# K and V tiles of a cached-attention decode block: from 4 heads by 32 token groups to 32 heads by 4 token quarters

## The chip, the cores and the metric

The kernel runs on one core of a Trainium2 chip. The metric is the device time of one execution, in microseconds (us).

## The reference, cut to what matters

Two sequences, one new token each, pass through an adaptive layer norm, attention over a cached window of 1024 tokens with 32 heads of 192, an output projection, a second layer norm and a gated feed-forward block. All inputs are bf16.

```python
mod = (silu(c) @ w_mod).reshape(2, 6, 1, 640)               # shifts, scales, gates
h = layernorm(x) * (1 + ca) + sa
q = (h @ wq).reshape(2, 1, 32, 192)
k = k_cache[:, :, 3072:4096, :]                             # (2, 32, 1024, 192)
v = v_cache[:, :, 3072:4096, :]
p = softmax(q k^T * 192 ** -0.5)
x = x + ga * ((p v) @ wo)
h = layernorm(x) * (1 + cb) + sb
x = x + gb * ((gelu(h @ w_gate) * (h @ w_up)) @ w_down)
```

K and V are 25.2 MB each, the weights 26.5 MB. Every byte is used once.

## The kernel before

All loads are issued in a fixed order on one DMA queue, and each waits until its landing place is free. K and V land in a ring of 8 slots of 12 KB per partition. A tile holds 4 heads; each head has 32 partitions, and each partition holds 32 consecutive tokens, which lie in memory as one run of 32 x 192 x 2 = 12,288 B.

```python
HQ = 4; PH = P // HQ; J = W // PH            # 4 heads, 32 partitions each, 32 tokens
NQD = H // HQ; NG = B * NQD                  # 16 groups of (4 heads, one batch)
SLOT = J * Dh                                # 6144 elements = 12,288 B

def ring_src(it):                            # the source of a K or V tile
    # (cut)
    src = A_k_cache if kind == "k" else A_v_cache
    return src[b].rearrange("(i u) s d -> u i s d", u=NQD)[quad, :, K0:Sk, :] \
                 .rearrange("i (p j) d -> p i (j d)", p=PH), SLOT     # (shortened)
```

For each of the 16 groups, DVE multiplies K by the broadcast query in two chunks, PE sums over channels by multiplying with the identity, DVE finishes the sums, and a softmax follows: maximum, transpose, broadcast to 4 head columns, exponential, denominator. The four columns are a masked copy of the weights, one column per head, so PV can be a matmul with 8 weight columns (2 tokens x 4 heads); four such matmuls run side by side in column tiles of 32.

```python
S.op("dve", tensor_tensor(prod[...], ring[:, sl, chunk], qbc[...], mult))        # K * q
S.op("pe",  matmul(bank, lhsT=ident_b, rhs=prod[...]))                           # 6 per chunk
# (cut: maximum, transpose, broadcast)
S.op("act", activation(E_sb[:, z, :, :], Sb_sb, Exp, scale=SCALE, accum_out=denp))
for jp in range(NPAIR):                                                          # PV
    i = jp % NR
    e.matmul(ps[32 * i:32 * i + 2 * HQ, BK_O, 0:ON],
             lhsT=E_sb[:, z, 2 * jp:2 * jp + 2, :], rhs=ring[:, sl, 2 * jp * Dh:(2 * jp + 2) * Dh],
             tile_position=(0, 32 * i))
```

The code above is shortened; the whole kernel follows.

Of the kernel before, what the change touches and what calls it, by code (L numbers as in the profile page):

```python
# [119 lines left out]
def bass_adaLN_cond__sliding_block_cached__geglu_ffn__decode_kernel(  # L120
# [24 lines left out]
    HQ = 4  # L145
    PH = P // HQ
    J = W // PH
    NQD = H // HQ
    NG = B * NQD
# [4 lines left out]
    assert B == 2 and D == KT * P and J * PH == W and NQD * HQ == H and NT * P == NQ  # L154
    assert DD * NT == Dh and DD * H == P and NR * FR == FC and FC * P == F and DR == KT * 32
    assert HQ == NR and DD * NQD == 32
    SCALE = float(Dh) ** -0.5
    EPS = 1e-5
    NEG = 1e30
    JC = 16  # L160
    NCK = J // JC
    GC = 512 // JC
    NCH = Dh // GC
    assert GC * NCH == Dh and NCK == 2
    ON = 2 * Dh
    NPAIR = J // 2

    NS = 8
    SLOT = J * Dh
    WQ_SPLIT = [(0, 2), (2, 3)]  # L170
    WO_SPLIT = [(0, 28), (28, 17), (45, 3)]
    NWQ, NWO = len(WQ_SPLIT), len(WO_SPLIT)
# [4 lines left out]
    HP = P // 2  # L177
    X0 = DD * NQD - 1
    ZW = X0 + P
# [3 lines left out]
    assert NQB * QW == NQD * Dh  # L183
# [3 lines left out]
    with es:  # L187
# [3 lines left out]
        ring = sb("ring", [P, NS, SLOT], BF16)  # L191
        R3N = max(KT * 6 * D, 2 * KT * F + FC * D)
        r3 = sb("r3", [P, R3N], BF16)
        wm_v = r3[:, 0:KT * 6 * D].rearrange("p (k n) -> p k n", k=KT)
        wg_v = r3[:, 0:KT * F].rearrange("p (k n) -> p k n", k=KT)
        wu_v = r3[:, KT * F:2 * KT * F].rearrange("p (k n) -> p k n", k=KT)
        wd_v = r3[:, 2 * KT * F:2 * KT * F + FC * D].rearrange("p (f n) -> p f n", f=FC)
        prod = sb("prod", [P, 4, JC, Dh], BF16)
        qbc = sb("qbc", [P, B, NQD * Dh], BF16)
# [5 lines left out]
        mask_h = sb("mask_h", [P, HQ], F32)  # L205
        bcL = sb("bcL", [1 + HQ, P], F32)
        bcR = sb("bcR", [1 + HQ, 2, HQ], F32)
# [4 lines left out]
        selq = sb("selq", [P, B, P], BF16)  # L212
        ztmp = sb("ztmp", [P, NR, 2, HQ], BF16)
# [16 lines left out]
        S_sb = sb("S_sb", [P, 2, J], F32)  # L230
        Sb_sb = sb("Sb_sb", [P, 2, J, HQ], F32)
        M1 = sb("M1", [P, 2], F32)
        E_sb = sb("E_sb", [P, 2, J, HQ], BF16)
        denp = sb("denp", [P, 2], F32)
        rden = sb("rden", [P, 2], F32)
        On = sb("On", [P, 2, B, ON], BF16)
# [21 lines left out]
        sem_wm = S.sem("d_wm")  # L258
        sem_wg = S.sem("d_wg")
        sem_wu = [S.sem("d_wu%d" % i) for i in range(len(WU_SPLIT))]  # L260
        sem_wd = [S.sem("d_wd%d" % i) for i in range(len(WD_SPLIT))]
        sem_ring = [S.sem("d_ring%d" % i) for i in range(NS)]
# [5 lines left out]
        items = [("wq", k) for k in range(NWQ)]  # L268
        items += [("k", 0)]
        for g in range(1, NG):  # L270
            items += [("k", g), ("v", g - 1)]
        items += [("v", NG - 1)]
        items += [("wo", i) for i in range(NWO)]
        nslots = {("wq", i): -(-n * NQ // SLOT) for i, (_, n) in enumerate(WQ_SPLIT)}
        nslots.update({("wo", i): -(-n * D // SLOT) for i, (_, n) in enumerate(WO_SPLIT)})
        slot_of, before_of, pos = {}, {}, 0
        holder = [None] * NS
        for it in items:
            m = nslots.get(it, 1)
            assert pos + m <= NS  # L280
            slot_of[it] = pos
            before_of[it] = [holder[z] for z in range(pos, pos + m) if holder[z] is not None]
            for z in range(pos, pos + m):
                holder[z] = it
            pos = (pos + m) % NS
        ring_f = ring[:, :, :].rearrange("p s n -> p (s n)")
        ring_state = {"next": 0, "done": set()}

        def ring_key(it):
            return [("ring", z) for z in range(slot_of[it], slot_of[it] + nslots.get(it, 1))]  # L290

        def group(g):
            return divmod(g, B)

        def ring_src(it):
            kind, i = it
            if kind == "wq":
                k0, n = WQ_SPLIT[i]
                return A_wq.rearrange("(p k) n -> p (k n)", k=KT)[:, k0 * NQ:(k0 + n) * NQ], n * NQ
            if kind == "wo":  # L300
                t0, n = WO_SPLIT[i]
                return A_wo.rearrange("(p t) n -> p (t n)", t=NT)[:, t0 * D:(t0 + n) * D], n * D
            quad, b = group(i)
            src = A_k_cache if kind == "k" else A_v_cache
            return src[b].rearrange("(i u) s d -> u i s d", u=NQD)[quad, :, K0:Sk, :].rearrange("i (p j) d -> p i (j d)", p=PH), SLOT

        def declare_ring(consumed=()):
            ring_state["done"].update(consumed)
            while ring_state["next"] < len(items):
                it = items[ring_state["next"]]  # L310
                if not all(h in ring_state["done"] for h in before_of[it]):
                    break
                src, width = ring_src(it)
                o0 = slot_of[it] * SLOT
                S.dma("sp", k_dma(ring_f[:, o0:o0 + width], src), sem_ring[slot_of[it]], writes=ring_key(it), name="ld_%s%d" % it)
                ring_state["next"] += 1

        wm_dma = S.dma("sp", k_dma(wm_v.rearrange("p k n -> p (k n)"), w_mod.rearrange("(p k) n -> p (k n)", k=KT)), sem_wm,
                       writes=["wm"], name="ld_wm")
        declare_ring()  # L320
# [3 lines left out]
        for nm, t in (("scT", scT), ("oT", oT), ("aT", aT)):  # L324
# [16 lines left out]
             reads=["ones_b"], writes=["selg"], name="selg")  # L341
        for b in range(B):
            S.op("pool", lambda e, b=b: e.affine_select(out=selq[:, b, :].rearrange("p (x h) -> p x h", h=HQ),
                                                        in_=ones_b[:, 0:1].unsqueeze(2).broadcast_to([P, PH, HQ]),
                                                        pattern=[[0, PH], [-32, HQ]],
                                                        compare_op=ALU.is_equal, fill=0.0, base=-b, channel_multiplier=1),
                 reads=["ones_b"], writes=[("selq", b)], name="selq%d" % b)
        S.op("pool", lambda e: e.affine_select(out=ztmp[:, :, :, :].rearrange("p i q h -> p i (q h)"),
                                                in_=ones_b[:, 0:1].unsqueeze(2).broadcast_to([P, NR, 2 * HQ]),
                                                pattern=[[-32, NR], [-1, 2 * HQ]],  # L350
                                                compare_op=ALU.is_equal, fill=0.0, base=0, channel_multiplier=1),
             reads=["ones_b"], writes=["ztmp"], name="ztmp")
        S.op("pool", lambda e: e.memset(zsel[:, :, :], 0.0), writes=["zsel"], name="zsel0")
        S.op("pool", lambda e: e.memset(bcL[:, :], 1.0), writes=["bcL"], name="bcL1")
        S.op("pool", lambda e: e.affine_select(out=bcL[:, :].rearrange("k (x h) -> k x h", h=HQ),
                                                in_=ones_f[0:1 + HQ, :].rearrange("k (x h) -> k x h", h=HQ),
                                                pattern=[[0, PH], [-1, HQ]],
                                                compare_op=ALU.is_equal, fill=0.0, base=-1, channel_multiplier=1),
             reads=["ones_f", "bcL"], writes=["bcL"], name="bcLh")
        S.op("pool", lambda e: e.memset(bcL[0:1, :], 1.0), writes=["bcL"], name="bcL0")  # L360
        S.op("pool", lambda e: e.memset(bcR[:, :, :], -NEG), writes=["bcR"], name="bcRn")
        S.op("pool", lambda e: e.affine_select(out=bcR[:, :, :], in_=bcR[:, :, :],
                                                pattern=[[0, 2], [-1, HQ]],
                                                compare_op=ALU.not_equal, fill=0.0, base=-1, channel_multiplier=1),
             reads=["bcR"], writes=["bcR"] + [("bcR", z) for z in range(2)], name="bcRd")

        S.op("dve", lambda e: e.memset(ps[:, 0:4, :], 0.0), writes=[bank(k) for k in range(4)], name="init_Q")
        S.op("dve", lambda e: e.memset(ps[:, 5:8, :], 0.0), writes=[bank(k) for k in range(5, 8)], name="init_O")
# [41 lines left out]
        def ln_mod(tag, opc_idx, s_idx, dst_bf):  # L410
# [7 lines left out]
            def f(e):  # L418
                last = None
                hv = hrow[:, :].rearrange("p (m j) -> p m j", j=KT)  # L420
                for j in range(KT):
                    for i in range(NR):
# [10 lines left out]
             reads=["mask_h"], writes=["maskc"], name="maskc")  # L433
        S.op("dve", lambda e: e.tensor_reduce(out=zsel[:, :, X0:X0 + P].rearrange("p q (h m) -> p q h m", m=32)[:, :, :, 0],
                                              in_=ztmp[:, :, :, :].rearrange("p i q h -> p q h i"), axis=AX.X, op=ALU.max),
             reads=["ztmp", "zsel"], writes=["zsel"], name="zsel")

        mod_pe = []
        for half in range(2):
# [143 lines left out]
        for g in range(NG + 2):  # L583
# [6 lines left out]
            if pp:  # L590
                c_rec(g - 2)
# [147 lines left out]
```

## Time and profile before

| | kernel before |
|---|---|
| time | 188.15 us median of 3 runs (188.1 to 188.38) |
| bytes moved | 77.03 MB |
| K and V | 32 transfers of 1536 KB |
| packets of K and V in the trace | 4096 of 12,288 B, mean 464.3 ns each |

First, lines of the page of the kernel before: the span, busy time by engine, the DMA rows of the 40 equal slices of the span (busy tenths, then GB/s), the packet total, and the shares of the chain of work that ended last.

```profile
span 186.7 us, 2408 instructions
...
PE 106.9 (57%) x1038; PEld 51.9 (28%) x1039; DVE 98.2 (53%) x147; ACT 30.0 (16%) x72; POOL 5.1 (3%) x23
...
DMA  8989998999999999999999999999999999999991
GB/s 296 486 366 437 474 422 379 437 427 427 429 424 427 417 426 432 424 424 425 421 427 427 427 430 421 420 429 424 429 422 424 449 462 422 404 402 428 408 399 51
DMA packets 6518, 77.03 MB, mean 413 GB/s; under 512 B 746, under 2 KB 876, under 8 KB 1516
...
DMA 72%; DVE 16%; PE 5%; ACT 2%; SPq 1%; issue 1%
```

The 16 DMA engines are busy in every slice but the last, so the kernel is bound by its DMA stream. No engine is busy for more than 57% of the span. Next, stretches of time of the same kernel; the columns are the stretch, its length, busy time (and instructions) of PE, PE's weight loads, DVE, ACT and POOL, then the granted clock, the DMA share and GB/s. From 13 to 20 us the first part of wq lands; from 45 to 145 us K and V stream.

```profile
13.00:20.00 7.00, 4.60 (x62) 1.84 (x62) 2.22 (x11) 2.25 (x5) 0.00 (x0) 1.00 1.03 442
45.00:145.00 100.00, 67.93 (x518) 32.88 (x520) 75.85 (x99) 13.21 (x41) 0.00 (x0) 0.96 1.01 425
```

In a short stretch the rate is blurred by packets that cross its edges. Cutting the packets at the edges, by their times in the trace, gives 432.7 GB/s for 13 to 20 us and 425.2 for 45 to 145.

Three groups of instructions of the kernel before (busy time, mean ns of one, then idle time before them and what ended it): the K products, the PV matmuls, and the scaling of the PV result.

```profile
L490 DVE TENSOR_TENSOR prod<-ring,qbc 128x3072 bf16<-128x3072 bf16 x32 | 55.9, 1752 | 16.1 <-DMA ring<-in_A_k_cache_dram 16.1
...
L563 ACT ACTIVATE On<-ps,rden 128x384 bf16<-128x384 f32 x16 | 9.3, 581 | 42.4 <-DVE rden L561 31.9
L551 PE MATMUL ps<-ring,E_sb 128*8 128x384 bf16 x256 | 14.8, 356 | 0.0
```

DVE sits idle for 16.1 us before its K products, waiting for K to land. Last, how K and V are issued (count, size, time from issue to landing), and the moment when the output projection starts (start, duration, instruction, and in brackets what it waited for).

```profile
ring<-in_A_k_cache_dram SPq DMA_DIRECT2D x16, 1536.0 KB, 24.6
ring<-in_A_v_cache_dram SPq DMA_DIRECT2D x16, 1536.0 KB, 24.8
```

```profile
162.24 3.92 PE L622 MATMUL ps<-ring,oT 128*17 128x160 bf16 x112 [2.93 <-DMA ring<-in_A_wo_dram]
```

The output projection waits for its weights, not for attention.

### The profile page before, as it was taken

To read this page: it belongs to the slowest core of one execution; us is meant where nothing else is said; L and a number is where in the kernel's file an instruction comes from. 1 tells how busy PE (TensorE), PEld (TensorE's weight loads), DVE (VectorE), ACT (ScalarE), POOL (GpSimd) and SP (SyncE) were. 2 spreads that over 40 slices of the span, in tenths; PEclk is the share of its full clock that TensorE was granted. 3 is DMA by queue.
4 is the path that set the end of the run, shared out by engine and by line. 5 is a ranking of instruction groups with operands and counts; after the bars stand their busy time and mean duration, and the time that the engine had idled before them with its cause. 6 is when DMAs were issued, how large, how long until landed. Compare 5 with 4: busy or idle time off the path is not lost.

```text
span 186.7 us, 2408 instructions
## 1 busy us (share of the span) xinstructions
PE 106.9 (57%) x1038; PEld 51.9 (28%) x1039; DVE 98.2 (53%) x147; ACT 30.0 (16%) x72; POOL 5.1 (3%) x23
## 2 busy tenths in 40 slices
PE   0015710833876678656649656665576895356472
PEld 0011200211243333322314313333233252355321
DVE  6114000019788889587596595785865934002311
ACT  2022100091020212021012011110110103100610
POOL 8200000000000000000000000000000000000000
PEclk9999999997899999999996999999998558555567
DMA  8989998999999999999999999999999999999991
GB/s 296 486 366 437 474 422 379 437 427 427 429 424 427 417 426 432 424 424 425 421 427 427 427 430 421 420 429 424 429 422 424 449 462 422 404 402 428 408 399 51
DMA packets 6518, 77.03 MB, mean 413 GB/s; under 512 B 746, under 2 KB 876, under 8 KB 1516
## 3 DMA queue, kind: packets, MB, share of 16 engines
q1 hardware_dynamic: 6492, 76.88, 97.6%
q8 instruction: 8, 0.13, 0.3%
q14 instruction: 2, 0.02, 0.0%
q10 hardware_dynamic: 16, 0.01, 0.0%
HBM read 76.88 MB, written 0.00 MB: 412 GB/s over the span
## 4 chain that ended last, share of the span: by engine, by line
DMA 72%; DVE 16%; PE 5%; ACT 2%; SPq 1%; issue 1%
DMA ring<-in_A_k_cache_dram 38%; DMA ring<-in_A_wq_dram 17%; DMA r<-in_B_w_down_dram 17%; DVE prod L490 10%; DVE S_sb L509 4%; PE ps L502 2%; PE ps L467 2%; ACT qbc L483 2%; SPq L266 1%; DVE ps L485 1%; DVE M L512 1%; ACT qrow L474 1%; DVE bcR L519 0%; PE ps L526 0%; PE ps L684 0%
## 5 line engine op out<-in xcount | busy, mean ns | idle before, releaser
L490 DVE TENSOR_TENSOR prod<-ring,qbc 128x3072 bf16<-128x3072 bf16 x32 | 55.9, 1752 | 16.1 <-DMA ring<-in_A_k_cache_dram 16.1
L502 PE MATMUL ps<-prod,ident_b 128*128 128x512 bf16 x192 | 51.5, 411 | 15.7 <-DVE prod L490 15.6
L502 PEld LDWEIGHTS ps<-prod,ident_b 128*128 128x128 bf16 x192 | 17.2, 102 | 40.3 <-DVE prod L490 21.0
L509 DVE TENSOR_REDUCE S_sb<-ps 128x32 f32<-128x1024 f32 x16 | 19.3, 1206 | 0.9 <-PE ps L502 0.9
L526 PE MATMUL ps<-bcR,bcL 5*128 5x4 f32 x32 | 6.3, 264 | 22.3 <-DVE bcR L519 22.3
L563 ACT ACTIVATE On<-ps,rden 128x384 bf16<-128x384 f32 x16 | 9.3, 581 | 42.4 <-DVE rden L561 31.9
L551 PE MATMUL ps<-ring,E_sb 128*8 128x384 bf16 x256 | 14.8, 356 | 0.0
L534 ACT ACTIVATE E_sb<-Sb_sb 128x128 bf16<-128x128 f32 x16 | 5.0, 311 | 57.6 <-DVE Sb_sb L531 57.6
L467 PE MATMUL ps<-ring,hT 128*2 128x512 bf16 x60 | 6.7, 626 | 9.9 <-DMA ring<-in_A_wq_dram 9.0
L526 PEld LDWEIGHTS ps<-bcR,bcL 5*128 5x128 f32 x32 | 4.9, 190 | 26.3 <-DVE bcR L519 26.3
L622 PE MATMUL ps<-ring,oT 128*17 128x160 bf16 x192 | 6.8, 338 | 5.5 <-DMA ring<-in_A_wo_dram 5.5
L477 DVE CAST qrow<-ps 128x512 bf16<-128x512 f32 x1 | 0.7, 692 | 15.8 <-PE ps L467 15.8
L531 DVE TENSOR_TENSOR Sb_sb<-S_sb,ps 128x128 f32<-128x128 f32 x16 | 4.6, 289 | 7.8 <-PE ps L526 7.8
L540 PEld LDWEIGHTS ps<-denp,maskc 128*128 128x128 f32 x32 | 6.9, 218 | 3.6 <-ACT E_sb L534 0.9
L622 PEld LDWEIGHTS ps<-ring,oT 128*17 128x17 bf16 x192 | 6.1, 135 | 6.1 <-DMA ring<-in_A_wo_dram 6.1
L641 DVE TENSOR_TENSOR lnt<-ps,modR 128x160 f32<-128x160 f32 x1 | 0.3, 325 | 13.6 <-PE ps L622 13.6
L551 PEld LDWEIGHTS ps<-ring,E_sb 128*8 128x8 bf16 x256 | 5.0, 87 | 3.2 <-issue 0.7
L467 PEld LDWEIGHTS ps<-ring,hT 128*2 128x2 bf16 x60 | 1.7, 114 | 14.9 <-DMA ring<-in_A_wq_dram 9.9
L540 PE MATMUL ps<-denp,maskc 128*128 128x1 f32 x32 | 5.0, 226 | 0.8 <-ACT E_sb L534 0.8
L383 PE MATMUL ps<-ident_b,crow 2*128 2x2 bf16 x5 | 0.4, 177 | 8.2 <-DMA crow<-in_c_dram 8.2
L576 PE MATMUL ps<-On,zsel 128*128 128x96 bf16 x64 | 4.6, 223 | 0.7 <-ACT On L563 0.7
L514 PE MATMUL ps<-ident_f,M 128*1 128x128 f32 x16 | 4.5, 280 | 0.4 <-DVE M L512 0.4
(81 smaller groups left out, 71.5 us busy)
## 6 DMA issues: line engine op xcount, KB each, us to landing
ring<-in_A_k_cache_dram SPq DMA_DIRECT2D x16, 1536.0 KB, 24.6
ring<-in_A_v_cache_dram SPq DMA_DIRECT2D x16, 1536.0 KB, 24.8
r<-in_w_mod_dram SPq DMA_DIRECT2D x1, 4800.0 KB, 14.1
ring<-in_A_wq_dram SPq DMA_DIRECT2D x1, 4608.0 KB, 32.0
ring<-in_A_wo_dram SPq DMA_DIRECT2D x1, 4480.0 KB, 24.6
ring<-in_A_wq_dram SPq DMA_DIRECT2D x1, 3072.0 KB, 20.6
ring<-in_A_wo_dram SPq DMA_DIRECT2D x1, 2720.0 KB, 23.0
r<-in_B_w_gate_dram SPq DMA_DIRECT2D x1, 1920.0 KB, 25.1
```

The lines of the kernel that those rows point to most:

```text
L467: last = e.matmul(ps[32 * i:32 * i + B, n, :], lhsT=hT[:, k, :], rhs=wv[:, kk, i, n * QW:(n + 1) * QW], start=(k == 0), stop=(k == KT - 1) ...
L490: S.op("dve", lambda e: e.tensor_tensor(out=prod[:, 2 * (g % 2) + ci, :, :], in0=ring[:, sl, ci * JC * Dh:(ci + 1) * JC * Dh].rearrange("p ...
L502: last = e.matmul(o_ap, lhsT=ident_b[:, :], rhs=prod[:, pz, :, t * GC:(t + 1) * GC], start=(t == 0), stop=(t == NCH - 1))
L509: S.op("dve", lambda e: e.tensor_reduce(out=S_sb[:, z, :], in_=ps[:, 2 * z:2 * z + 2, :].rearrange("p k (j c) -> p (k j) c", c=GC), axis=A ...
L526: S.op("pe", lambda e: e.matmul(ps[:, BK_T, P:P + HQ], lhsT=bcL[:, :], rhs=bcR[:, z, :], start=True, stop=True), reads=[("bcR", z), "bcL"] ...
L531: S.op("dve", lambda e: e.tensor_tensor(out=Sb_sb[:, z, :, :], in0=S_sb[:, z, :].unsqueeze(2).broadcast_to([P, J, HQ]), in1=ps[:, BK_T, P: ...
L534: S.op("act", lambda e: e.activation(out=E_sb[:, z, :, :], in_=Sb_sb[:, z, :, :], func=ACTF.Exp, scale=SCALE, accum_out=denp[:, z:z + 1]), ...
L540: S.op("pe", lambda e: e.matmul(ps[:, BK_T, P + 16:P + 17], lhsT=maskc[:, :], rhs=denp[:, z:z + 1], start=True, stop=True), reads=[("denp" ...
L551: last = e.matmul(ps[32 * i:32 * i + 2 * HQ, BK_O, 0:ON], lhsT=E_sb[:, z, 2 * jp:2 * jp + 2, :].rearrange("p j h -> p (j h)"), rhs=ring[:, ...
L563: S.op("act", lambda e: e.activation(out=On[:, quad % 2, b, :], in_=ps[:, BK_O, 0:ON], func=ACTF.Identity, scale=rden[:, z:z + 1]), reads= ...
L576: last = e.matmul(ps[:, BK_OT, 0:B * NT].rearrange("p (b t) -> p b t", b=B), lhsT=zsel[:, jj, x:x + P], rhs=On[:, quad % 2, :, jj * Dh + d ...
L622: last = e.matmul(ps[32 * i:32 * i + RM, BK_M, 0:DR], lhsT=oT[:, t, :], rhs=wv[:, tl, i, :], start=(t == 0), stop=(t == NT - 1), tile_posi ...
```

## The change

The intent is to feed the DMA engines longer runs. All 32 heads now sit side by side with 4 partitions each, and a partition holds a quarter of the window, 256 tokens. A tile is 64 tokens of each quarter, one run of 24,576 B per partition, and a batch is 4 K tiles and 4 V tiles. Everything else follows from that layout: there is one softmax per batch, over 256 columns; the weights for PV are expanded with a mask to 32 columns, one per head, so that a PV matmul has 64 weight columns and only two column tiles run side by side; and since slots of 24 KB and the weights no longer fit apart, one arena of 6 slots holds everything, and w_mod, wq, wo and the feed-forward weights share it with K and V.

```diff
-    HQ = 4
-    PH = P // HQ
-    J = W // PH
-    NQD = H // HQ
-    NG = B * NQD
+    XQ = P // H
+    J = W // XQ
+    TT = 64
+    NTL = J // TT
+    SLOT = TT * Dh
@@ where tiles land
-        ring = sb("ring", [P, NS, SLOT], BF16)
-        r3 = sb("r3", [P, R3N], BF16)
+        NS = 6
+        NAR = NS * SLOT
+        arena = sb("arena", [P, NAR], BF16)
+        place = {("wm", 0): (0, KT * 6 * D), ("wq", 0): (2 * SLOT, wq_n[0]), ("wq", 1): (2 * SLOT + wq_n[0], wq_n[1])}
+        tiles = [("k", 0, t) for t in range(NTL)] + [("v", 0, 0)]
+        for t in range(NTL):
+            tiles += [("k", 1, t)] + ([("v", 0, t + 1)] if t + 1 < NTL else [])
+        tiles += [("v", 1, t) for t in range(NTL)]
+        for n, it in enumerate(tiles):
+            place[it] = ((n + NS - 1) % NS * SLOT, SLOT)
@@ source of a tile
-            return src[b].rearrange("(i u) s d -> u i s d", u=NQD)[quad, :, K0:Sk, :].rearrange("i (p j) d -> p i (j d)", p=PH), SLOT
+            return src[b][:, K0:Sk, :].rearrange("h (x j) d -> h x j d", x=XQ)[:, :, t * TT:(t + 1) * TT, :].rearrange("h x j d -> h x (j d)")
@@ weights of PV (new on DVE) and PV
+                S.op("dve", lambda e, z=z, j0=j0: e.tensor_tensor(out=Em[:, z, :, :], in0=E_sb[:, b, j0:j0 + JE].unsqueeze(2).broadcast_to([P, JE, H]),
+                                                                  in1=maskE[:, :].unsqueeze(1).broadcast_to([P, JE, H]), op=ALU.mult),
-                    last = e.matmul(ps[32 * i:32 * i + 2 * HQ, BK_O, 0:ON],
-                                    lhsT=E_sb[:, z, 2 * jp:2 * jp + 2, :].rearrange("p j h -> p (j h)"),
+                        last = e.matmul(ps[64 * i:64 * i + 2 * H, BK_O, 0:ON],
+                                        lhsT=Em[:, z, 2 * jp:2 * jp + 2, :].rearrange("p j h -> p (j h)"),
... (cut: the softmax per batch, the query broadcast, the selection of the result, bookkeeping)
```

## The prediction

> **What bounds the kernel now: the DMA stream.** The page shows 77.03 MB at a mean of 413 GB/s; the DMA row of the 40 slices stands at 8 or 9 tenths until the last slice. By stretches, 45 to 145 us (K and V streaming) has DMA share 1.01 at 425 GB/s, while DVE is busy 75.9 of 100 us and PE 67.9. The chain of waits is 72% DMA. DVE idles 16.1 us for K landings. Only the first microsecond and the tail after the last w_down landing (183.5 to 186.7 us) are not DMA.
>
> **What the change does to the DMA.** Bytes stay. K and V go from 32 transfers in 4096 packets of 12,288 B to 16 transfers in (I expect) 2048 packets of 24,576 B. The trace has both sizes: a 12,288 B packet takes 460 to 473 ns, mean 464.3; the 128 packets of 24,576 B of the first wq part take 912 ns each, and their stretch (13 to 20 us) runs at 432.7 GB/s. 50.33 MB at 425.2 GB/s is 118.4 us; at 431 to 432.7 it is 116.3 to 116.8. Estimate: 1.6 to 2.1 us less, all on the critical path, since wo, gate, up and down shift forward with it.
>
> **What could give it back.** Partitions now walk 32 heads, 1.5 MB apart, instead of four contiguous head blocks. The Trainium skill ("DMA: Bandwidth & Descriptors", Latency and other measured facts) lists row pitches of large powers of two that slow HBM copies, 512 KiB mildly, 2 MiB strongly. No stretch of this trace has a 1.5 MB pitch; I keep one chance in four that packets take 1 to 4% longer than 912 ns.
>
> **Does the shared arena starve the queue?** I count not. At 7.3 us a tile, K/V runs from 31 to 148 us. DVE per K tile: 4 products of 1752 ns and 2 sums of 1206 ns, 9.4 us. Queries are ready near 40.5 us (first product now at 43.0; 6 query copies of 613 ns become 2 short ones, a 1.34 us memset goes), so batch 0's K ends near 79 us, its softmax near 83. Tightest reuses: V0 tile 0's slot is free near 90, wanted near 104; K1 tile 0's near 100, wanted near 111. The slots of w_mod and wq are free near 20, 24 and 37 us, before wanted.
>
> **Computation.** Removed: 16 groups' max, transpose, broadcast, subtract, exp, denominator and On (On alone 9.3 us of ACT), replaced by 2. Added: 8 expanded-weight products of 2048 elements; a broadcast operand may hold DVE to one element a cycle, about 2.1 us each (estimate, at the 0.96 GHz of "Trainium Kernel Development and Optimization", NeuronCore Architecture), 17 us in all. PV keeps 256 matmuls of 384 columns, but two column tiles run side by side instead of four: estimate twice the 14.8 us of PE busy time. All off the path. The last V tile should finish PV, selection and oT near 157 us, before wo's first part lands near 160 (162.2 now).
>
> **Prediction.** 186.4 us; range 185.2 to 189.5. Faster by over 2%: 0.06; within 2%: 0.83; slower by over 2%: 0.11.
>
> **Right or wrong in the profile.** Right: 24,576 B packets near 912 ns; 45 to 140 us at 430 to 433 GB/s; DMA row without gaps; wo's first matmul about 2 us earlier; DVE still idle for landings late in the stream. Wrong: K/V packets above 930 ns (address pattern); dips in the DMA row (starved reuse: long waits of the DMA queue just before them); wo's first matmul waiting for oT, not its DMA; a lower granted clock stretching the last feed-forward chain past the last landing.

## More of the kernel before

Executions of one kernel here agree within about 0.3%, and differences of a few tenths of a microsecond are read from several rounds on one chip, with the kernel before run beside each experiment. The experiments ran on three chips; a comparison across chips leans on the kernel before, whose median was 188.15 to 188.21 us on each.

## The result, and the profile after

The kernel after takes 186.85 us (median of 4 runs, 186.81 to 187.10), beside 188.25 us for the kernel before in the same rounds. The ratio is 0.9929, 95% interval 0.9911 to 0.9946: a little faster, well within 2%. A ratio here is the mean time of one kernel's runs over that of the other's runs of the same rounds, so it is not quite the ratio of the medians quoted. Executions over 1.5% slower than the fastest of the same kernel are left out of the means.

The page of the kernel after, in the lines shown of before:

```profile
span 185.6 us, 2065 instructions
...
PE 105.1 (57%) x923; PEld 48.5 (26%) x923; DVE 105.1 (57%) x98; ACT 14.2 (8%) x26; POOL 6.4 (3%) x23
...
DMA  9989999999999999999999999999999999999991
GB/s 331 440 375 450 461 433 403 434 434 424 424 434 424 434 445 434 422 429 429 426 434 424 424 440 422 424 445 440 429 429 429 441 418 456 398 404 421 408 390 38
DMA packets 4213, 77.01 MB, mean 415 GB/s; under 512 B 491, under 2 KB 621, under 8 KB 1261
...
DVE 41%; DMA 35%; PE 21%; SPq 1%; issue 1%; ACT 1%
```

There are 2305 packets fewer, the DMA row is still full to the last slice, PE is about as busy as before and DVE 7 us more. The chain of work now says DVE 41% and DMA 35%, where it said DMA 72%. That is not a new bottleneck. The chain is followed back through what released each DMA issue, often the last reader of a slot; but other transfers were in flight at that moment, and the DMA row shows no gap. A chain through a prefetch names who freed the slot, not who set the pace.

The long stretch, in the kernel after:

```profile
45.00:145.00 100.00, 64.49 (x323) 26.71 (x321) 81.02 (x59) 1.78 (x5) 0.00 (x0) 0.89 1.00 430
```

K and V stream at 430 GB/s in place of 425. The groups that answer to those shown of before, and the expanded weights, which are new:

```profile
L498 DVE TENSOR_TENSOR prod<-arena,qbc 128x3072 bf16<-128x3072 bf16 x32 | 54.7, 1750 | 2.7 <-DMA arena<-in_A_k_cache_dram 2.7
...
L561 PE MATMUL ps<-arena,Em 128*64 128x384 bf16 x256 | 26.1, 369 | 7.1 <-DVE Em L547 7.1
...
L547 DVE TENSOR_TENSOR Em<-E_sb,maskE 128x2048 bf16<-128x2048 bf16 x8 | 18.2, 2283 | 2.8 <-PE ps L561 2.8
...
L568 ACT ACTIVATE On<-ps,rden 128x384 bf16<-128x384 f32 x2 | 1.2, 581 | 57.0 <-PE ps L561 57.0
```

The PV matmuls keep PE busy for 26.1 us in place of 14.8, the new weights cost DVE 18.2 us (8 of 2283 ns), and 14 of 16 scalings of the result are gone. DVE now waits only 2.7 us for K. The issues, and the start of the output projection:

```profile
arena<-in_A_k_cache_dram SPq DMA_DIRECT2D x8, 3072.0 KB, 32.1
arena<-in_A_v_cache_dram SPq DMA_DIRECT2D x8, 3072.0 KB, 23.8
```

```profile
158.87 0.52 PE L595 MATMUL ps<-On,zsel 128*128 128x96 bf16 x8 [0.68 <-ACT On L568]
161.16 2.12 PE L611 MATMUL ps<-arena,oT 128*17 128x160 bf16 x112 [1.77 <-DMA arena<-in_A_wo_dram]
```

The projection starts 1.08 us earlier (162.24 to 161.16) and still waits for its weights. The selection of attention's result ran at 158.87 us, so attention ended only about 1 us before the weights landed.

So the gain can be placed. The first K packet starts at 31.14 us before and at 31.19 after. The first packet of wo starts at 149.05 us before and at 147.97 after. From there on both kernels keep the same distance: the output store is issued at 184.94 and at 183.83. From the first K packet to the first of wo it is 117.91 us before and 116.78 after, so the gain is inside the K and V stream. (These two profiled executions differ by 1.11 us, the medians by 1.40: the profiled one of before took 187.95 us, under its three other runs.) The experiments ask what in that stream gave it.

### The profile page after: what moved, and what is told of

It is laid out like the page before. It is cut to its first block, busy times and chain, and to the rows that moved or that the text cites. A ratio compares the mean times of both kernels' runs of the same rounds, so it can differ in the third digit from the quotient of the medians.

```text
span 185.6 us, 2065 instructions
## 1 busy us (share of the span) xinstructions
PE 105.1 (57%) x923; PEld 48.5 (26%) x923; DVE 105.1 (57%) x98; ACT 14.2 (8%) x26; POOL 6.4 (3%) x23
## 4 chain that ended last, share of the span: by engine, by line
DVE 41%; DMA 35%; PE 21%; SPq 1%; issue 1%; ACT 1%
DVE prod L498 23%; DMA arena<-in_A_k_cache_dram 21%; DMA arena<-in_B_w_down_dram 14%; PE ps L510 11%; DVE S_sb L517 10%; PE ps L561 8%; DVE Em L547 6%; SPq L282 1%; DVE negm L527 1%; ACT E_sb L535 1%; PE ps L538 1%; PE ps L531 1%; DVE M L523 0%; PE ps L661 0%; PE ps L525 0%
## 5 line engine op out<-in xcount | busy, mean ns | idle before, releaser
L498 DVE TENSOR_TENSOR prod<-arena,qbc 128x3072 bf16<-128x3072 bf16 x32 | 54.7, 1750 | 2.7 <-DMA arena<-in_A_k_cache_dram 2.7
L510 PEld LDWEIGHTS ps<-prod,ident_b 128*128 128x128 bf16 x192 | 17.8, 104 | 57.4 <-DVE prod L498 37.5
L561 PE MATMUL ps<-arena,Em 128*64 128x384 bf16 x256 | 26.1, 369 | 7.1 <-DVE Em L547 7.1
L517 DVE TENSOR_REDUCE S_sb<-ps 128x32 f32<-128x1024 f32 x16 | 19.5, 1221 | 14.4 <-PE ps L510 14.4
L561 PEld LDWEIGHTS ps<-arena,Em 128*64 128x64 bf16 x256 | 15.7, 124 | 17.0 <-DVE Em L547 9.1
L547 DVE TENSOR_TENSOR Em<-E_sb,maskE 128x2048 bf16<-128x2048 bf16 x8 | 18.2, 2283 | 2.8 <-PE ps L561 2.8
L472 PE MATMUL ps<-arena,hT 128*2 128x512 bf16 x60 | 6.6, 615 | 10.0 <-DMA arena<-in_A_wq_dram 9.0
L611 PE MATMUL ps<-arena,oT 128*17 128x160 bf16 x192 | 5.0, 276 | 6.2 <-DMA arena<-in_A_wo_dram 6.2
L611 PEld LDWEIGHTS ps<-arena,oT 128*17 128x17 bf16 x192 | 4.4, 109 | 6.5 <-DMA arena<-in_A_wo_dram 6.5
L568 ACT ACTIVATE On<-ps,rden 128x384 bf16<-128x384 f32 x2 | 1.2, 581 | 57.0 <-PE ps L561 57.0
L450 PE MATMUL ps<-arena,scT 128*17 128x480 bf16 x40 | 4.3, 596 | 0.3 <-DMA arena<-in_w_mod_dram 0.3
L632 PE MATMUL ps<-arena,h2T 128*2 128x384 bf16 x40 | 3.8, 484 | 0.6 <-DMA arena<-in_B_w_up_dram 0.3
## 6 DMA issues: line engine op xcount, KB each, us to landing
arena<-in_A_wq_dram SPq DMA_DIRECT2D x1, 3072.0 KB, 20.6
```

The lines of the kernel that those rows point to most:

```text
L450: last = e.matmul(ps[32 * i:32 * i + RM, half, 0:MH].rearrange("p (m n) -> p m n", n=DR), lhsT=scT[:, k, :], rhs=wv[:, 3 * half:3 * half + ...
L472: last = e.matmul(ps[32 * i:32 * i + B, n, :], lhsT=hT[:, k, :], rhs=wv[:, kk, i, n * QW:(n + 1) * QW], start=(k == 0), stop=(k == KT - 1) ...
L498: S.op("dve", lambda e: e.tensor_tensor(out=prod[:, pz, :, :], in0=view(("k", b, t), lo, JC * Dh).rearrange("p (j d) -> p j d", d=Dh), in1 ...
L510: last = e.matmul(o_ap, lhsT=ident_b[:, :], rhs=prod[:, pz, :, t * GC:(t + 1) * GC], start=(t == 0), stop=(t == NCH - 1))
L517: S.op("dve", lambda e: e.tensor_reduce(out=S_sb[:, b, 2 * JC * pair:2 * JC * (pair + 1)], in_=ps[:, 2 * z:2 * z + 2, :].rearrange("p k (j ...
L547: S.op("dve", lambda e, z=z, j0=j0: e.tensor_tensor(out=Em[:, z, :, :], in0=E_sb[:, b, j0:j0 + JE].unsqueeze(2).broadcast_to([P, JE, H]), ...
```

## The experiments

### Which part of the change gives the time: five kernels

The theory was packet length: a packet costs a fixed few ns beside its bytes. Its rivals were the number of transfers (16 in place of 32), the walk over 32 heads 1.5 MB apart, and the computation taken away. The first kernel keeps the layout and all computation of after, and only fetches each tile in two transfers, each with half of every run. (The diffs of the experiments are shortened where they show "...".)

```diff
-                queue["ops"][it] = S.dma("sp", k_dma(view(it), source(it)), sem_of[it], writes=keys(it), ...)
+                    for hf in range(2):
+                        n2 = SLOT // 2
+                        S.dma("sp", k_dma(view(it, hf * n2, n2), source(it)[:, :, hf * n2:(hf + 1) * n2]), sem_hf[it][hf], ...)
```

> The kernel after, with every K and V tile fetched by two transfers of 12,288 B runs instead of one of 24,576 B; heads, order, arena and computation stay. Packet length theory (each packet costs a fixed 8 ns or so besides its bytes, read from the shortest packets of both traces: 460, 912 and 1364 ns for 12,288, 24,576 and 36,864 B): 2048 more packets x 8 ns / 16 engines = 1.0 us, and 16 more completion packets of 9 ns per engine, 0.14 us: about 188.0 to 188.3 us, the time before, K/V packets 464 ns. Rival, address pattern (32 heads instead of 4 blocks is what changed the rate): stays at 186.9. Rival, removed computation (the gain is the 16 softmax groups): stays at 186.9.

The next ones replace the source by one contiguous block of 3 MB a tile, so that a gap in the landing place can cut the runs while the transfer stays one. Their results are wrong. (The comparison with the reference accepted them all the same. It is thus no test of the attention part. To make room, e_flat_12k and e_flat_6k also put the gelu output into memory of the scores.)

```diff
-            return src[b][:, K0:Sk, :].rearrange("h (x j) d -> h x j d", x=XQ)[:, :, t * TT:(t + 1) * TT, :].rearrange("h x j d -> h x (j d)")
+            return src[b].rearrange("h s d -> (h s d)")[t * P * TT * Dh:(t + 1) * P * TT * Dh].rearrange("(p n) -> p n", p=P)     # e_flat_24k
+            ... .rearrange("(p c n) -> p c n", p=P, c=NPC)     # e_flat_12k: NPC = 2, e_flat_6k: NPC = 4; landing place with a gap after each piece
```

> Wrong result on purpose: the kernel after, but every K and V tile reads one contiguous block of 3 MB instead of 128 runs spread over 32 heads; one transfer of 24,576 B packets as after. Packet length theory: 186.85 plus or minus 0.2 us and packets of 916 ns on the mean, as after. Address theory: the packets change, to 912 ns if the 32-head walk costs something (0.3 to 0.5 us less), or above 920 ns if it helps.

> Wrong result on purpose: as e_flat_24k, one transfer of 3 MB per tile, but a gap of 128 B in each partition's landing place cuts the runs to 12,288 B. Packet length theory: 1.0 to 1.2 us over e_flat_24k, about 187.9 to 188.1. Transfer count theory (the gain came from 16 transfers fewer, their starts and completions): same as e_flat_24k, 186.9.

> Wrong result on purpose: as e_flat_12k with runs of 6,144 B, 8192 packets, still 16 transfers. Packet length theory: 6144 more packets than 24,576 B runs x 8 ns / 16 = 3.1 us, up to 3.6 with the few ns that packets lose under load: 190.0 to 190.5 us. Transfer count theory: 186.9.

The last one came after the others. It fetches the contiguous blocks in two transfers of 12,288 B runs, which separates the number of transfers from the address walk.

> Wrong result on purpose: contiguous 3 MB blocks as in e_flat_12k (187.50 us), but each fetched by two transfers of 12,288 B runs as in e_two_transfers (188.11 us). It closes the gap between these two, which differed in the address walk as well as in the number of transfers. If the number of transfers is worth the 0.61 us between them: 188.0 to 188.2 us, packets at 464 ns. If the address walk over 32 heads is what cost it with 12,288 B runs: 187.5 us, packets at 462 ns.

Measured, 5 runs each; the kernel before had medians of 188.21 us beside the first four and 188.18 beside the last. The packet column is the mean over all K and V packets in the trace.

| kernel | addresses | transfers | run, B | packet, ns | time, us | ratio to before (95%) |
|---|---|---|---|---|---|---|
| before | 4 head blocks | 32 | 12,288 | 464.3 | 188.21 | |
| e_two_transfers | 32 heads | 32 | 12,288 | 464.2 | 188.11 | 0.9994 (0.9981 to 1.0006) |
| e_flat_two | 3 MB block | 32 | 12,288 | 464.4 | 188.10 | 0.9992 (0.9978 to 1.0005) |
| e_flat_12k | 3 MB block | 16 | 12,288 | 462.0 | 187.50 | 0.9961 (0.9947 to 0.9974) |
| e_flat_24k | 3 MB block | 16 | 24,576 | 916.2 | 186.89 | 0.9930 (0.9918 to 0.9943) |
| after | 32 heads | 16 | 24,576 | 916.2 | 186.85 | 0.9929 (0.9911 to 0.9946) |
| e_flat_6k | 3 MB block | 16 | 6,144 | 236.4 | 189.44 | 1.0063 (1.0050 to 1.0076) |

The stretch from 45 to 145 us of e_two_transfers, e_flat_12k, e_flat_24k and e_flat_6k, in this order:

```profile
45.00:145.00 100.00, 63.88 (x324) 26.36 (x323) 82.12 (x60) 1.78 (x5) 0.00 (x0) 0.89 1.01 426
```

```profile
45.00:145.00 100.00, 63.47 (x345) 27.01 (x345) 83.85 (x60) 1.78 (x5) 0.00 (x0) 0.93 1.01 428
```

```profile
45.00:145.00 100.00, 63.46 (x345) 27.06 (x345) 83.71 (x60) 1.78 (x5) 0.00 (x0) 0.93 1.00 430
```

```profile
45.00:145.00 100.00, 63.62 (x326) 26.49 (x324) 82.16 (x59) 1.78 (x5) 0.00 (x0) 0.92 1.02 421
```

The last column goes 426, 428, 430, 421 GB/s, with PE, DVE and ACT busy alike. The ranges of the runs of e_flat_24k, e_flat_12k and e_flat_two (186.79 to 187.09, 187.38 to 187.60, 188.01 to 188.31) do not meet. Four things follow.

- With two transfers a tile the whole gain is gone, though the layout, the softmax per batch and the expanded weights are all still there. Those are worth 0.10 us by the medians, which the interval (0.36 us gained to 0.11 us lost) does not tell from nothing. The removed computation gave no time that shows.
- The walk over heads costs nothing that shows: e_flat_24k and the kernel after differ by 0.04 us, and e_flat_two and e_two_transfers by 0.01.
- Longer packets at the same number of transfers give 187.50 - 186.89 = 0.61 us. Each engine handles 128 packets fewer, so one packet costs 4.8 ns beside its bytes. (The gap that cuts the runs does not itself lengthen a packet: the commonest time of a 12,288 B packet is 460 ns with it and, in e_flat_two, without.) With 6,144 B runs it is (189.44 - 186.89) / 384 packets = 6.6 ns. The expectation took 8 ns from the shortest packets, and was too high; successive packets of an engine overlap by 4 ns in the trace (the start of one is 3 or 4 ns before the end of the last), which that fit had left out.
- Fewer transfers at the same packet length give 188.10 - 187.50 = 0.60 us. For 16 transfers that is 37.5 ns each. The expectation had counted only the completion packet (4 B, one per engine and transfer) of 9 ns, 0.14 us in all, and this is the larger miss. The two kernels ran on different chips; e_two_transfers, on the chip of e_flat_12k, gives 0.61 us. A rival goes with it: two transfers of half runs also fetch each 24,576 B in two passes, so no packet continues at the address where the last one ended. No kernel was made to part the two. The kernel before speaks against the rival: its 32 transfers run through their blocks in order, and it has the packets (464.3 ns) and the time (188.21 us) of the kernels that skip; and after, whose packets skip from head to head, is as fast as e_flat_24k.

### Where the cost of a transfer sits, and whether computation has a part in it

In the trace of after, the packets of 24,576 B take 912 ns without exception while wq lands, and nearly so until about 42 us, then 916 ns on the mean. Computation on K starts at 40.6 us, so contention was a natural suspect. Three kernels cut the computation and leave every transfer alone; their results are wrong.

```diff
# e_light_dve and e_light_both: K products on 2 of 16 tokens (prod is filled with zeros once)
-            tensor_tensor(out=prod[:, pz, :, :],   in0=view(("k", b, t), lo, JC * Dh)..., in1=qbc[...] over JC tokens
+            tensor_tensor(out=prod[:, pz, 0:2, :], in0=view(("k", b, t), lo, 2 * Dh)...,  in1=qbc[...] over 2 tokens
# e_light_pe and e_light_both: reductions on 2 of 16 tokens, 4 of 32 PV matmuls
-                    last = e.matmul(o_ap, lhsT=ident_b[:, :], rhs=prod[:, pz, :, t * GC:(t + 1) * GC], ...)
+                    last = e.matmul(o_ap[:, 0:2], lhsT=ident_b[:, :], rhs=prod[:, pz, 0:2, t * GC:(t + 1) * GC], ...)
-                    for jp in range(JE // 2):
+                    for jp in (0, 1, JE // 2 - 2, JE // 2 - 1):
```

> Wrong result on purpose: the kernel after with 2 of 16 tokens per K product and per K reduction, and 4 of 32 PV matmuls per V tile; all transfers as after. In the trace after, 24,576 B packets take exactly 912 ns until computation starts near 42 us and 916 on the mean from then on. Contention theory (DVE or PE reading the landing memory lengthens each packet by about 4 ns): packets back at 912 to 913 ns throughout, K/V stretch at 432 to 433 GB/s, about 0.5 us less, 186.3 us. Rival (the lengthening comes with the K/V stream itself, or with queue depth): packets stay at 916 ns and the time at 186.85.

> Wrong result on purpose: only the PE part of that cut (reductions and PV); DVE products stay whole. If PE's reads cause the longer packets: 912 to 913 ns and about 186.3 us. If DVE's do: 915 to 916 ns and 186.8.

> Wrong result on purpose: only the DVE K products cut to 2 of 16 tokens; PE stays whole. If DVE's reads cause the longer packets: 912 to 913 ns and about 186.3 us. If PE's do: 915 to 916 ns and 186.8.

Measured: e_light_both 186.99 us (186.74 to 187.20), e_light_pe 187.08 (186.76 to 187.27), e_light_dve 186.80 (186.70 to 186.98), with mean packets of 916.1, 916.1 and 916.2 ns. From 45 to 145 us in e_light_both:

```profile
45.00:145.00 100.00, 20.55 (x206) 12.92 (x206) 46.67 (x60) 1.78 (x5) 0.00 (x0) 0.50 1.01 431
```

PE is busy for 20.6 us in place of 64.5, DVE for 46.7 in place of 81.0, and the stream runs at 431 GB/s as against 430. My contention theory falls. The Trainium skill ("SBUF — State Buffer", SBUF: two separate sides) says that engine ports and DMA ports are disjoint and that a compute operation cannot slow a DMA; these three runs agree. Nor was any of them faster than the kernel after beyond 0.05 us (their ratios to before are 0.9926 to 0.9939, that of after 0.9929), so computation sets no time here. (The granted clock was about 0.63 in two of these profiles, and the time stayed.)

What the lengthening does follow is the number of transfers. Between 45 and 145 us I summed by how much each packet exceeds the usual shortest of its size (234, 460, 912 or 1815 ns; at most 16 ns are counted, so that a handful of long ones do not weigh) and divided by the completion packets:

| kernel | run, B | transfers of K and V | lengthening per completion packet |
|---|---|---|---|
| before | 12,288 | 32 | 31 ns |
| e_two_transfers | 12,288 | 32 | 32 ns |
| e_flat_12k | 12,288 | 16 | 26 ns |
| after | 24,576 | 16 | 28 ns |
| e_mixed_48k (below), runs of 49,152 B | 49,152 | 6 of 10 | 25 ns |
| e_flat_6k | 6,144 | 16 | 70 ns |

At 12,288 B and above, a transfer costs each engine 9 ns for its own completion packet and 25 to 32 ns in slightly longer packets, spread over the stream. Nine plus 28 is 37 ns, which agrees with the 37.5 ns from the times. The 6,144 B row does not fit. Why packets lengthen with the number of transfers, and why the first ones are free of it, stays open: no run here separates the causes.

### Twice the transfers with the same packets: a miss

To double the transfers without touching the packets, each tile was fetched as two sets of 16 heads.

```diff
+                    for hf in range(2):
+                        S.dma("sp", k_dma(view(it)[64 * hf:64 * (hf + 1), :], source(it)[16 * hf:16 * (hf + 1)]), sem_hf[it][hf], ...)
```

> The kernel after with every K and V tile fetched by two transfers of 16 heads (64 partitions) each: packets stay 2048 of 24,576 B, transfers go back to 32. From the runs so far, packets and transfers would each have given 0.6 us of the gain (12,288 B runs with 16 transfers cost 0.61 us over 24,576 B runs, two transfers a tile another 0.61). Half-and-half theory: about 187.4 to 187.5 us, K/V packets near 920 ns on the mean. Rival (packet length alone counts, and the 0.61 us of the split came from interleaving two halves of the same rows): 186.9 us. If 64 partitions do not spread evenly over the 16 engines, the time is far above both.

Measured: 305.54 us (300.52 to 306.45), far above both theories; four of the six runs count as slow beside the fastest, the profiled one among them, a spread of 2% that does not matter beside the size of the effect. The DMA rows of its page:

```profile
DMA  9999999999999999999999999999999999999994
GB/s 369 416 429 457 213 219 219 213 210 213 213 210 209 229 213 210 213 213 207 210 226 213 210 216 210 213 207 210 223 216 209 219 213 210 227 411 397 421 412 166
```

The DMA row stands at 9 tenths in every slice but the last, and through K and V the rate is half. In the trace about 16 packets are in flight at any time, as before, but each takes 1843 ns on the mean in place of 916. The Trainium skill ("SBUF — State Buffer", Door 1: The DMA port swizzle) has a reason that fits: partitions 0 to 63 reach 8 of the 16 ports on the DMA side, with a limit near 218 GB/s, and partitions 64 to 127 the other 8. This run's stream was 213 GB/s from 45 to 145 us, so the page and the trace agree, though no run here parts the ports from other effects of a transfer of 64 partitions. The run says nothing about the cost of a transfer, and leaves the rival of half runs where it was. e_flat_two, which came after it, settles the address walk, not that rival.

### Going further: runs of 49,152 B

> A correct kernel that goes further: K and V tiles of 128 tokens per quarter, runs of 49,152 B, 8 transfers of 6 MB, three slots of 48 KB. Packet length theory: 1024 packets fewer than after x 8 ns / 16 = 0.5 us, plus 8 completions of 9 ns, plus 4 ns of contention per packet if that is per packet (0.26 us): 186.0 to 186.4 us, provided the three slots don't starve the queue (tightest reuse about 4 us ahead of its need by my count). If they do starve it, dips in the DMA row and 187 us or more. Transfer count theory: the loss of 8 transfers alone is under 0.1 us.

```diff
-    TT = 64
+    TT = 128
-        NS = 6
+        NS = 3                                             # slots of 48 KB
+        BASE = [0, SLOT, KT * 6 * D + KT * NQ]             # the last one beside w_mod and wq
```

(The gelu output was also moved into memory of the scores, to fit, here and in e_mixed_48k below. By the author's account, two other kernels that were to put a gap into the head layout were never run, because their address patterns could not be expressed in one transfer; the record holds nothing of them.)

Measured: 189.89 us (189.22 to 190.34), ratio to before 1.0089 (1.0071 to 1.0107): slower than both. The DMA queue's own instructions in e_48k (start, duration), and its DMA rows:

```profile
86.44 0.54 SPq L283 DMA_DIRECT2D arena<-in_A_v_cache_dram  x1
103.25 0.54 SPq L283 DMA_DIRECT2D arena<-in_A_k_cache_dram  x1
117.80 8.19 SPq L283 DMA_DIRECT2D arena<-in_A_v_cache_dram  x2
```

```profile
DMA  8989999989989899897999898999998999999980
GB/s 286 483 372 465 471 388 416 502 387 450 481 356 502 366 471 481 356 485 345 493 418 429 335 460 370 377 429 450 408 460 387 440 433 412 431 395 431 410 339 19
```

The transfers ahead of these were due to run out near 89.5, 104 and 118.7 us (31.3 us plus four, five and six times 14.56 us), so they were issued 3, 1 and 1 us before they were needed. The first packets of each then took about 2000 to 2750 ns in place of 1815, and near 104.6 us only 5 packets were in flight where 16 are usual. The rate from 45 to 145 us is 423 GB/s. Three large slots starve the queue; I had counted about 4 us of lead and the last two had a quarter of it.

> A correct kernel that goes on from the last one without its late slots: batch 0's K stays in four transfers of 24,576 B runs, all other tiles go in six transfers of 49,152 B runs, 10 transfers and 1280 packets in place of 16 and 2048. By the measured terms (4.6 to 4.8 ns per packet and engine: 48 packets, 0.22 us; 37 ns per transfer and engine: 6, 0.22 us) about 0.4 us under the kernel after, 186.4 to 186.5 us, with no dips in the DMA row. Rival (the shared slots starve the queue again): 187 us or more, packets over 2000 ns at the start of a transfer.

```diff
+        def span(kind, b):
+            return TT if (kind, b) == ("k", 0) else 2 * TT      # only batch 0's K in tiles of 64 tokens
+        for it, z in zip(tiles, (4, 5, 0, 1, 2, 4, 0, 2, 4, 0)):
+            place[it] = (BASE[z], span(*it[:2]) * Dh)
```

Measured: 186.49 us (186.37 to 186.62, 4 runs, correct), ratio to before 0.9911 (0.9896 to 0.9925). The same queue in e_mixed_48k, and its DMA row:

```profile
80.59 0.54 SPq L282 DMA_DIRECT2D arena<-in_A_v_cache_dram  x1
96.49 0.53 SPq L282 DMA_DIRECT2D arena<-in_A_k_cache_dram  x1
111.04 8.19 SPq L282 DMA_DIRECT2D arena<-in_A_v_cache_dram  x2
```

```profile
DMA  8989999999999989899898989899998999999991
```

Here the three transfers were issued 9, 8 and 8 us ahead of need, only three of the 768 packets of 49,152 B took over 1830 ns, and from 33 to 148 us never fewer than 15 packets were in flight. The last K or V packet landed at 149.54 us, against 152.48 in e_48k: those 2.9 us are about the whole difference between the two profiled executions. The expectation of a row without dips failed, though: 8s stand in it throughout the stream, without a starved queue. With packets of 49,152 B they are no sign of one; the packets in flight are. The time is 0.36 us under the median of after, where 0.4 had been expected from 48 packets and 6 transfers fewer per engine. It was not run in the same rounds as the kernel after, but the ranges of the two do not meet. This version beats both kernels, by 0.9% over before.

## Why the prediction was right, and where its sum was off

The time, 186.85 us, lies in the range of 185.2 to 189.5 and 0.45 us above the predicted 186.4; "within 2%" had 0.83. The range also holds 188.15, the time before, so lying in it proves no mechanism. Point by point:

- **"What bounds the kernel now: the DMA stream"** holds. With PE at a third and DVE at 58% of their busy time the run is no faster (e_light_both), and a change to the transfers alone takes the gain away (e_two_transfers).
- **"50.33 MB at 425.2 GB/s is 118.4 us; at 431 to 432.7 it is 116.3 to 116.8"** was right in kind, and the saving was mis-sized. After, the stream from the first K packet to the first of wo lasted 116.78 us (431.0 GB/s), the upper edge of what was said. Before, it lasted 117.91 us (426.9 GB/s), not 118.4: the rate of 45 to 145 us was used for the whole stream, which starts faster (428.6 GB/s from 31.5 to 45 us). So the saving was 1.13 us, and the projection's first matmul came 1.08 us earlier in place of "about 2 us". The upper rate, 432.7, was too high as well: the wq stretch is a single transfer, so no other transfer's costs are in it, and its packets are all at 912 ns. The K and V packets after are at 916.2.
- **The cause was half of what I thought.** The prediction gave the whole gain to the size of the packets. Packet length gave 0.61 us (4.8 ns for each of 128 packets per engine) and the number of transfers 0.60 us (37.5 ns for each of 16). The prediction named "32 transfers" and "16 transfers" and gave that no term. That its sum came so near is partly luck: it compared the rates of two stretches, and these hold the cost of the transfers unnamed beside that of the packets.
- **"One chance in four that packets take 1 to 4% longer than 912 ns"** because of the 1.5 MB pitch did not come about: a contiguous block (e_flat_24k) has the same packets and the same time.
- **"Does the shared arena starve the queue? I count not"** was right, with less room than I counted. Batch 0's softmax ended near 90.4 us, where I had 83, because each sum on DVE waits for PE's reductions (DVE idles 14.4 us before the sums, where it idled 0.9 us before), which I had not counted. The issue of V0's tile 3, shown below, came at 98.07 us, for a transfer due near 104.3 (31.2 us plus ten tiles of 7.31): 6 us of room where I had 14. The e_48k run shows what happens when such room falls to 1 to 3 us.
- **"All off the path"** was right for the computation. The new weights took 2283 ns each (estimate 2.1 us), PV 26.1 us (estimate 29.6), and DVE's total is 105.1 us where it was 98.2. "The last V tile should finish PV, selection and oT near 157 us" (oT is attention's result as the projection reads it) came out at 160.0 us, 1.2 us before the weights landed; a batch 1 slower by more than that would have been on the path.
- **"DVE still idle for landings late in the stream"**, one of the signs that were to be right, did not come about: the 2.7 us that DVE waits for K all lie before its first product, at 40.56 us. From then on K was always there before DVE wanted it, which goes with the loss of room in the fifth point.

The lines for the fifth point, from the timeline of the kernel after: the first expanded weights of batch 0, which start when its softmax has ended, and the issue of V0's tile 3.

```profile
90.37 2.27 DVE L547 TENSOR_TENSOR Em<-E_sb,maskE 128x2048 bf16<-128x2048 bf16 x1
...
98.07 0.54 SPq L282 DMA_DIRECT2D arena<-in_A_v_cache_dram  x1
```

## What to carry to other kernels

When the DMA row is full, count packets and transfers per engine and price both from the trace: here 4.8 ns for a packet and 37.5 ns for a transfer, so that halving both gave 1.2 us of 188, and rearranged computation gave nothing. Take a rate from a stretch with the same number of transfer boundaries as the one to be predicted, not from the cleanest stretch, and take the time before of a whole stream from its first and last packets. Larger tiles pay only while each slot comes free several microseconds before the queue needs it: runs of 48 KB lost 1.7 us over before with 1 to 3 us of lead and won 1.7 us with 8.

## What the Trainium skill lacked or had wrong

- "SBUF — State Buffer", The DMA setup-cost knee, gives every transfer a roughly fixed 2 us. For the whole cost of one more transfer in a queue that never runs dry, no page has a figure: the runs show 37.5 ns per transfer (188.10 against 187.50 us for 16 transfers more), of which 9 ns are the completion packet.
- "DMA: Bandwidth & Descriptors", Why small descriptors are slow, finds joining of consecutive descriptors worth it only at 256 B or less. No run here joins descriptors; longer runs make fewer of them, and in a stream that is bound by the DMA engines, going from 12,288 to 24,576 B still gave 0.61 us (4.8 ns a packet), and 6,144 B cost 2.55 us more than 24,576.
- "DMA: Bandwidth & Descriptors", Latency and other measured facts, lists slow row pitches of large powers of two between HBM tensors, and no page has a pitch such as 1.5 MB for loads: here it cost nothing (186.85 against 186.89 us for contiguous blocks).
- "SBUF — State Buffer", Door 1, is right about 64 partitions (213 GB/s here). It does not say how this looks in a profile: the DMA row stays full and 16 packets stay in flight, each at 1843 ns in place of 916. A full row alone does not show a full rate.
